# Queries through fp32 loads and on-chip DMA transposes, in an attention kernel followed by a mixture of adapters

## The chip, the cores and the metric

The kernel runs on one core of a Trainium2 chip. The metric is the device time of one execution in microseconds. Before the change the median of three runs is 381.16 us (380.85 to 381.24).

## The reference

```python
# q: 4 x 12288 x 128, kv: 4 x 384 x 32 x 128, w_sr: 128 x 128, all float32
kv_pool = kv.reshape(B, H // 4, 4, W // 4, 4, C).mean(axis=(2, 4))   # 768 keys per batch
k = v = kv_pool.reshape(B, -1, C) @ w_sr
s = (1 / sqrt(C)) * (q @ k.transpose(0, 2, 1))
a = exp(s - s.max(-1)); a /= a.sum(-1) + 1e-09
x = (a @ v).reshape(B * 12288, 128)

logits = x @ w_gate                       # 8 experts
topk = the 2 experts of largest logits
w = softmax of the two logits
delta = sum over the two experts e of w_e * ((x @ A[e]) @ B[e])      # rank 16
return x + delta                          # 49152 x 128, float32
```

## The kernel before, in words

The 49,152 query rows are cut into 96 chunks of 512 rows, 24 chunks a batch. A chunk lies on the chip as 128 partitions by 4 strips (`S`) of 128 columns. Four chunks make a group (`GT` = 2048 rows).

The work of a chunk is a chain. `scores` multiplies the turned queries `qT` (channels on the partitions) by the turned keys `kfT` in three units of two key blocks each (`sg`, in PSUM), and ScalarE takes the exponential into `em`. `attend` multiplies `em` by the values `vx`, which carry the seven differences of the expert logits and a column of ones beside them, into the single accumulator `acc`, one of the four strips at a time. `normalize` takes the reciprocal of the sums (L315) and writes the attention output `xn` (L320). `top` sorts the eight logits of each row on VectorE, `route` and `gates` make the gate weights `gw` on GpSimd, with one tanh on ScalarE between them. `transposes` turns `xn`, so that `down` can multiply by all eight A matrices at once (`h_ps`); `gate` multiplies by `gw` into `hg` on VectorE; `hg` is turned, `up` multiplies by B (`d_ps`), and `finish` adds `xn` and stores the rows.

The main loop (L547) runs over slots `k`, one a chunk, and every engine keeps the order in which the program names its instructions; so does the queue of SP, which issues most transfers. In slot `k` the kernel makes the scores of chunk `k`, attends chunk `k - 1`, normalizes chunk `k - 2`, and lets the chunk of the list `enter[k]` (four or so behind) go through `down` and `gate`. Slots 0 to 7 are an opening written out by hand as a string of steps (L525). Routing is done for two chunks at a time up to chunk 67, in every second slot, and for one chunk from then on.

Chunks up to 67 turn `xn` and `hg` on TensorE, one slot's pair in one PSUM tile `tt_ps`, copied by VectorE into `tts` (L389). Chunks 68 to 89 (`by_dma`) have both turned by one DMA transpose per slot on SP's queue (L407): GpSimd narrows `xn` to bf16 (L403), `gate` writes bf16 beside it, and the transpose takes the two from one tile `turn` to another, 8 blocks of 128 x 128.

Queries of the first eight chunks are loaded in fp32 and turned on TensorE (`load_q`, `turn_q`). For the others GpSimd issues a casting transfer of one group from HBM to HBM (`cast_q`, L80, 512 KB out), and later SP issues a DMA transpose of that group, 16 blocks, into the tile `qT` (`load_qT`, L90).

The keys of the next batch come in loads of 512 KB (`load_kv`, L102), one a slot, and GpSimd adds the 4 x 4 neighbours (`pool_step`, L221 and L223), three sums in every second slot. Then `prepare` turns the sums on TensorE, projects them and makes values and turned keys, one step in each of nine slots of a batch.

Three tiles `kvr` hold raw keys, eight tiles `osb` hold both the first queries and the outputs on their way, and two PSUM tiles `mb` are shared by `tt_ps`, `h_ps`, `d_ps` and the key work.

Of the kernel before, what the change touches and what calls it, by code (L numbers as in the profile page):

```python
# [10 lines left out]
FP32 = mybir.dt.float32  # L11
# [9 lines left out]
def kernel(  # L21
# [32 lines left out]
    qpool = ctx.enter_context(tc.tile_pool(name="qpool", bufs=4))  # L54
# [6 lines left out]
    qdram = ctx.enter_context(tc.tile_pool(name="qdram", bufs=1, space=bass.MemoryType.DRAM))  # L61
# [14 lines left out]
    q_bf, qT, kvr, spare = {}, {}, {}, {}  # L76

    def cast_q(g):
        t = qdram.tile([GT, C], BF16, tag=f"q{g}", name=f"qbf{g}")
        keep(nc.gpsimd.dma_start(t, q[g // NG, (g % NG) * GT:(g % NG + 1) * GT]))  # L80
        q_bf[g] = t

    def load_qT(g):
        if g < B * NG - GC:
            t = qpool.tile([P, GT], BF16, tag="qT", name="qT")
        else:
            if "q" not in spare:
                spare["q"] = kvpool.tile([P, 4, 2, 4 * C], FP32, tag="kvr", name="qTs")
            t = spare["q"][:, g % GC].rearrange("p x c -> p (x c)").bitcast(BF16)
# [17 lines left out]
    q_f = {}  # L107

    def load_q(g, m):
        q_f[g, m] = opool.tile([P, S, C], FP32, tag="osb", name="qf")  # L110
        src = q[0, g * GT:(g + 1) * GT].rearrange("(p j) c -> p j c", p=P)
        keep(nc.sync.dma_start(q_f[g, m], src[:, m * S:(m + 1) * S]))

    def turn_q(g, m, pool, engine):
        if m == 0:
            qT[g] = qpool.tile([P, GT], BF16, tag="qT", name="qT")
# [4 lines left out]
        for i in range(S):  # L121
            mm(ps[:, i], q_f[g, m][:, i], id_f, is_transpose=True,
               start=(i == 0), stop=(i == S - 1))
        o = qT[g][:, m * T:(m + 1) * T].rearrange("p (s t) -> p s t", s=S)
# [33 lines left out]
    for m in range(GC):  # L158
        load_q(0, m)
    load_first(1)  # L160
    load_first(2)
    for m in range(GC):
        load_q(1, m)
# [3 lines left out]
    keep(nc.sync.dma_start(a_f, moe_A.rearrange("e c r -> c e r")))  # L167

# [40 lines left out]

    def prepare(b, adder):  # L210
# [191 lines left out]
    def narrow(k, t):  # L402
        keep(nc.gpsimd.tensor_copy(strip(t, 0)[:, 0], xn[k][:, :, 0:C]))  # L403
# [427 lines left out]
```

## Time and profile before

| | |
|---|---|
| median of three runs | 381.16 us |
| profiled execution, first to last instruction | 379.1 us (its time otherwise is not given) |
| TensorE busy | 368.8 us, 97% |
| VectorE busy | 307.6 us, 81% |
| ScalarE busy | 293.3 us, 77% |
| GpSimd busy | 217.8 us, 57% |
| packets of SP's queue and of GpSimd's queue | 69.8% and 17.0% of 16 DMA engines' span |

Times inside the profile are microseconds from the first instruction. A row of a timeline has the start, the duration, the engine, the line of the kernel, the operation, what it writes and reads, how many instructions the row stands for, and in brackets how long the engine was idle before it and who ended that. PE is TensorE's matmul, PEld its weight load, DVE VectorE, ACT ScalarE, POOL GpSimd, SPq the queue of SP. The ends of matmuls are modelled, so a run of short ones is read from starts. A row of a group has busy time, mean duration in ns, and idle time before. Rows of DMA issues end with the median time from issue to landing.

### The profile page before, as it was taken

What the parts mean: (1) busy time and instruction counts of PE and PEld (TensorE: products, weight loads), DVE (VectorE), ACT (ScalarE), POOL (GpSimd) and SP (SyncE); (2) the same over time, 40 slices, a digit from 0 to 9 for tenths busy, and PEclk for the clock granted to TensorE, in tenths of its full rate; (3) what the DMA queues carried; (4) which work ended last, traced back from release to release, by engine and by line L of the source; (5) the groups of instructions that cost most, each with busy time, mean ns of one, the idle gap of its engine ahead of it and who ended that gap; (6) DMA issues with size and microseconds to landing.
All of it is one profiled execution on the core that took longest, in us unless ns stands there. A gap on an engine that the chain in (4) does not pass through costs nothing.

```text
span 379.1 us, 11473 instructions
## 1 busy us (share of the span) xinstructions
PE 368.8 (97%) x4448; PEld 292.5 (77%) x4448; DVE 307.6 (81%) x925; ACT 293.3 (77%) x368; POOL 217.8 (57%) x493
## 2 busy tenths in 40 slices
PE   8899999999999999999999999999999999999993
PEld 5577788788788887878788887878787777777782
DVE  1447799998989889898989888898988777777785
ACT  1448986776878788787878787777778999999873
POOL 0120468878732387777833267777675666666442
PEclk9999999999999999999999999999999999999998
DMA  7988979999999998997898998989955867777623
GB/s 247 388 291 151 279 184 266 340 224 241 152 213 228 299 278 268 255 235 165 171 201 226 288 239 245 306 233 198 217 137 140 169 163 153 150 205 168 141 86 140
DMA packets 93863, 82.22 MB, mean 217 GB/s; under 512 B 73104, under 2 KB 73872, under 8 KB 93456
## 3 DMA queue, kind: packets, MB, share of 16 engines
q1 hardware_dynamic: 92672, 69.75, 69.8%
q0 software_dynamic: 704, 11.54, 17.0%
q8 instruction: 35, 0.57, 0.6%
q10 hardware_dynamic: 432, 0.20, 0.2%
q14 instruction: 20, 0.16, 0.2%
HBM read 50.53 MB, written 36.70 MB: 230 GB/s over the span
## 4 chain that ended last, share of the span: by engine, by line
PE 91%; DMA 4%; DVE 2%; issue 1%; ACT 1%; SPq 0%; POOL 0%; ACTq 0%; DVEq 0%; POOLq 0%
PE acc L69 35%; PE sg L69 32%; PE tt_ps L69 8%; PE d_ps L69 5%; PE h_ps L69 5%; DMA kvr<-in_kv_dram 4%; PE kpT_ps L69 2%; PE v_ps L69 1%; DVE kvr L135 1%; DVE xn L320 1%; PE kfT_ps L69 1%; DMA out_dram<-osb 1%; PE qT_ps L69 0%; SPq L102 0%; PE tail_ps L69 0%
## 5 line engine op out<-in xcount | busy, mean ns | idle before, releaser
L294 ACT ACTIVATE em<-sg 128x1024 f16<-128x1024 f32 x288 | 282.4, 1022 | 66.8 <-PE sg L69 64.1
L69 PE MATMUL acc<-vx,em 128*128 128x136 f16 x2280 | 166.5, 223 | 0.0
L69 PEld LDWEIGHTS <-em 128*128 128x128 f16 x2304 | 145.2, 98 | 7.7 <-DVE xn L320 0.4
L69 PE MATMUL sg<-qT,kfT 128*128 128x512 bf16 x480 | 142.1, 379 | 0.8 <-ACT em L294 0.7
L320 DVE TENSOR_TENSOR xn<-acc,rinv 128x540 f32<-128x540 f32 x95 | 68.4, 720 | 3.3
L69 PEld LDWEIGHTS <-tts 128*128 128x128 bf16 x564 | 43.0, 98 | 31.6 <-issue 0.4
L223 POOL TENSOR_TENSOR kvr<-kvr 128x512 f32<-128x512 f32 x54 | 67.3, 1270 | 0.1
L352 POOL TENSOR_TENSOR over<-xn,srt 128x64 f32<-128x64 f32 (+1 forms) x120 | 30.9, 278 | 55.4 <-DVE srt L340 55.3
L433 DVE TENSOR_TENSOR osb<-d_ps,xn 128x512 f32<-128x512 f32 x91 | 62.5, 688 | 0.0
L420 DVE TENSOR_TENSOR hg<-h_ps,gw 128x512 bf16<-128x512 f32 x71 | 49.0, 691 | 6.3 <-POOL gw L368 1.2
L389 DVE COPY tts<-tt_ps 128x1024 bf16<-128x1024 bf16 (+1 forms) x73 | 49.0, 672 | 0.0
L69 PEld LDWEIGHTS <-kfT 128*128 128x128 bf16 x576 | 45.3, 98 | 2.7 <-issue 1.0
L315 DVE RECIPROCAL rinv<-acc 128x4 f32<-128x4 f32 x95 | 17.3, 182 | 36.9 <-PE acc L69 35.9
L367 POOL TENSOR_TENSOR gw<-th,over 128x64 f32<-128x64 f32 (+1 forms) x60 | 17.3, 288 | 49.6 <-ACT th L365 47.4
L69 PEld LDWEIGHTS <-xn 128*128 128x128 bf16 x296 | 22.5, 98 | 16.7 <-DVE xn L320 0.4
L340 DVE MAX8 srt<-xn 128x8 f32<-128x8 f32 x380 | 34.4, 152 | 0.1
L69 PE MATMUL sg<-qTs,kfT 128*128 128x512 bf16 x96 | 28.6, 379 | 0.0
L69 PE MATMUL tt_ps<-id_bf,xn 128*128 128x128 bf16 x284 | 27.4, 219 | 0.0
L69 PE MATMUL h_ps<-a_bf,tts 128*128 128x128 bf16 x284 | 27.4, 219 | 0.0
L69 PE MATMUL tt_ps<-id_bf,hg 128*128 128x128 bf16 x280 | 27.1, 219 | 0.0
L69 PE MATMUL d_ps<-b_bf,tts 128*128 128x128 bf16 x276 | 26.7, 219 | 0.1
L358 POOL TENSOR_SCALAR over<-over 128x64 f32<-128x64 f32 (+1 forms) x60 | 19.8, 330 | 5.4
(93 smaller groups left out, 280.7 us busy)
## 6 DMA issues: line engine op xcount, KB each, us to landing
out_dram<-osb SPq DMA_DIRECT2D x94, 256.0 KB, 4.3
kvr<-in_kv_dram SPq DMA_DIRECT2D x45, 512.0 KB, 7.8
qbf<-in_q_dram POOLq DMA_DIRECT2D x22, 512.0 KB, 7.7
qf<-in_q_dram SPq DMA_DIRECT2D x8, 256.0 KB, 7.4
kvr<-in_kv_dram SPq DMA_DIRECT2D x6, 256.0 KB, 7.8
out_dram<-osb SPq DMA_DIRECT2D x3, 128.0 KB, 2.3
turn<-turn SPq DMA_TRANSPOSE x23, 3.1
qT<-qbf SPq DMA_TRANSPOSE x18, 7.4
```

The costliest lines, as they stand in the source:

```text
L69: return keep(nc.tensor.matmul(*a, **k))
L223: keep(adder.tensor_tensor(u[:, lo:hi], u[:, lo:hi], v[:, lo:hi], op=ALU.add))
L294: keep(nc.scalar.activation(em[k][:, 2 * r:2 * r + 2], ps, AF.Exp, bias=0.0, scale=scale))
L315: keep(nc.vector.reciprocal(ri, acc[k][:, :, VC]))
L320: keep(nc.vector.tensor_tensor(x[:, :, 0:VC], acc[k][:, :, 0:VC], ri.unsqueeze(2).broadcast_to([P, S, VC]), op=ALU.mult))
L340: keep(nc.vector.max(srt[k0][:, m, s], xn[k][:, s, C:C + E]))
L352: keep(eng.tensor_tensor(d, lg, so[:, :, i].unsqueeze(2).broadcast_to([P, n, 8]), op=ALU.subtract))
L358: keep(eng.tensor_scalar(mask, mask, 0.0, None, op0=ALU.is_ge))
L367: keep(eng.tensor_tensor(w[:, 0:n], th, mask, op=ALU.mult))
L389: keep(nc.vector.tensor_copy(sb[:, lo:hi], ps[:, lo:hi]))
L420: keep(nc.vector.tensor_tensor(hg[k].rearrange("p s (e r) -> p (s e) r", e=E), hp[k].rearrange("p s (e r) -> p (s e) r", e=E), gw[k0][:, m ...
L433: keep(nc.vector.tensor_tensor(osb, dp[k], xn[k][:, :, 0:C], op=ALU.add))
```

## The change

Queries of all chunks are loaded as fp32, one chunk (256 KB) a transfer, seven slots ahead (`load_q(k + 7)`), into the `osb` tiles. In slot `k` GpSimd narrows the queries of chunk `k + 4` to bf16 into a tile `turn`, and SP turns them by a DMA transpose inside SBUF. From slot 13 on, `gate` also writes its result into that tile, so that one transpose of 8 blocks carries both; the turned `hg` is used by `up` three slots later. In the stage where `xn` was already turned by DMA, the same transpose now has 12 blocks. The casting transfers and the transposes out of HBM are gone, and so are the turns of `hg` on TensorE for the 59 chunks that enter in slots 13 to 71. The tiles for the turns are three sources and six targets in a pool of their own, and from slot 70 five of each inside two `kvr` tiles.

Keys of batches 2 and 3 come in pieces of 256 KB, one a slot from slot 16 to slot 63, with their sums one a slot two slots later (`add_piece`); keys of batch 1 stay as they were. The nine slots of `prepare` move for batches 2 and 3.

```diff
-    def cast_q(g):
-        t = qdram.tile([GT, C], BF16, tag=f"q{g}", name=f"qbf{g}")
-        keep(nc.gpsimd.dma_start(t, q[g // NG, (g % NG) * GT:(g % NG + 1) * GT]))
-        q_bf[g] = t
-
-    def load_qT(g):
...
-        keep(nc.sync.dma_start(t.rearrange("c (j p) -> c j p", p=P),
-                               q_bf[g].rearrange("(p j) c -> p (j c)", p=P), transpose=True))
-        qT[g] = t
...
+    def load_q(k):
+        g, m = k // GC, k % GC
+        q_f[k] = opool.tile([P, S, C], FP32, tag="osb", name="qf")
+        src = q[g // NG, g % NG * GT:(g % NG + 1) * GT].rearrange("(p j) c -> p j c", p=P)
+        keep(nc.sync.dma_start(q_f[k], src[:, m * S:(m + 1) * S]))
...
     def strip(t, i):
...
+        if (t, i) not in strips:
+            if t < TURN + 2:
+                strips[t, i] = tpool.tile([P, 2, S, C], BF16, tag=f"t{i}", name="turn", bufs=(3, 6)[i])
+            else:
...
+                strips[t, i] = spare[i][:, t % 5]
+        return strips[t, i]
 
-    def narrow(k, t):
-        keep(nc.gpsimd.tensor_copy(strip(t, 0)[:, 0], xn[k][:, :, 0:C]))
+    def narrow(t, at, src):
+        keep(nc.gpsimd.tensor_copy(strip(t, 0)[:, at], src))
 
-    def turn_dma(t, *what):
-        lo, hi = (0 if what[0][0] is xT or len(what) == 2 else 1), (2 if what[-1][0] is hgT else 1)
+    def turn_dma(t, lo, *what):
+        hi = lo + len(what)
         keep(nc.sync.dma_start(strip(t, 1)[:, lo:hi].rearrange("c h s p -> c (h s) p"),
                                strip(t, 0)[:, lo:hi].rearrange("p h s c -> p (h s c)"), transpose=True))
...
-    def cast_first():
-        keep(nc.gpsimd.tensor_copy(late, q_f[1, 2][:, 0, 0:1]))
-        for g in (2, 3):
-            cast_q(g)
-        for g in (2, 3):
-            load_qT(g)
+    def turn_pair(k):
+        for i in range(2):
+            narrow(k, i, q_f[k + i])
+        turn_dma(k, 0, (qT, k), (qT, k + 1))
...
+    pieces, adds = {}, {}
+    for b in range(2, B):
+        for n in range(24):
+            pieces[b * NB - 32 + n] = (b, n // 8, n % 8 // 2, n % 2)
...
     def begin(k):
...
+        if k in pieces:
+            load_kv(*pieces[k])
+        if k >= 5 and k + 7 < NCHUNK:
+            load_q(k + 7)
...
+    def add_piece(k):
+        b, h, r, x = pieces.get(k - 2, (0, 0, 0, 0))
+        if r > 0:
+            pool_step(b, h, r - 1, x)
+        for step in (3, 4):
+            b, h, r, x = pieces.get(k - step, (0, 0, 0, 0))
+            if r == 3 and x == 1:
+                pool_step(b, h, step, 0)
...
+    by_queue = [k for t in range(13, TURN + 4) for k in enter[t]]
+    late_up = {}
...
     for k in range(k1, NCHUNK):
...
+        kq = k + 4 if k + 4 < NCHUNK else None
...
         unit()
+        ku = ku + late_up.pop(k, [])
         if kx and not kd and all(x_ in by_dma for x_ in kx):
             down(kx[0])
             todo = []
             for n in kn:
                 normalize(n)
                 if n in by_dma:
-                    narrow(n, k)
-                    todo = [(xT, n)]
+                    narrow(k, 1, xn[n][:, :, 0:C])
+                    todo.append((xT, n))
             tanhs()
+            if kq is not None:
+                narrow(k, 0, q_f[kq])
+                todo.insert(0, (qT, kq))
...
             unit()
-            gate(kx[0], strip(k, 0)[:, 1])
+            gate(kx[0], strip(k, 0)[:, 2])
             todo.append((hgT, kx[0]))
             if len(kx) == 1:
-                turn_dma(k, *todo)
+                turn_dma(k, 3 - len(todo), *todo)
...
         tanhs()
+        todo = []
+        if kq is not None:
+            narrow(k, 0, q_f[kq])
+            todo.append((qT, kq))
...
         for x_ in kx[:1]:
             down(x_)
-            gate(x_)
+            if x_ in by_queue:
+                gate(x_, strip(k, 0)[:, 1 if k < TURN + 2 else 2])
+                todo.append((hgT, x_))
+                late_up[k + 3] = [x_]
+            else:
+                gate(x_)
+        if todo:
+            turn_dma(k, 0, *todo)
...
-        if b + 1 < B and i % 2 == 0 and (8 if b == 0 else 6) <= i <= 20:
-            for _ in range(4 if (b, i) == (0, 18) else 3):
+        add_piece(k)
+        if b == 0 and i % 2 == 0 and 8 <= i <= 20:
+            for _ in range(4 if i == 18 else 3):
                 sums.pop(0)()
```

In the opening, the step `late` (two casting transfers and two transposes out of HBM, for chunks 8 to 15) is replaced by `pair 8`, and a step `pair 10` is added before slot 2; the loads of the queries of chunks 8 to 11 follow the loads of the adapter weights.

More of the change, by code (lines that the diff above doesn't have):

```diff
@@ L167 @@
     keep(nc.sync.dma_start(a_f, moe_A.rearrange("e c r -> c e r")))
+    for k in range(2 * GC, 3 * GC):
+        load_q(k)
     warm = const.tile([P, 1], FP32)
@@ L227, in prepare @@
                 continue
-            sums.append([lambda h=h, step=step, lo=lo: pool_step(h, step, lo, lo + 512)
-                         for step in range(5) for lo in range(0, 1024 if step < 3 else 512, 512)])
+            sums.append([lambda h=h, step=step, x=x: pool_step(b, h, step, x)
+                         for step in range(5) for x in range(2 if step < 3 else 1)])
         st = {}
```

115 lines of the change are left out of this document (50 added, 65 removed), and 4 rows, old and new, of the table opening.

## The prediction

> **What bounds the kernel now.** I read the page first (busy shares, the chain that ended last, the DMA queues), then the timeline of single slots, then sums over three stretches.
>
> ```profile
> PE 368.8 (97%) x4448; PEld 292.5 (77%) x4448; DVE 307.6 (81%) x925; ACT 293.3 (77%) x368; POOL 217.8 (57%) x493
> PE 91%; DMA 4%; DVE 2%; issue 1%; ACT 1%; SPq 0%; POOL 0%; ACTq 0%; DVEq 0%; POOLq 0%
> q1 hardware_dynamic: 92672, 69.75, 69.8%
> q0 software_dynamic: 704, 11.54, 17.0%
> ```
>
> The chain is 91% TensorE and no other engine holds it for long; the two queues together fill 87% of the DMA engines' time, but they are off the chain after the opening. How much of TensorE's busy time is really path is read from starts, since the ends are modelled. Timeline of TensorE, a slot of the plain stage and one of the stage that already turns by DMA:
>
> ```profile
> 206.19 0.39 PE L69 MATMUL tt_ps<-id_bf,xn 128*128 128x128 bf16 x4
> 206.42 0.39 PE L69 MATMUL tt_ps<-id_bf,hg 128*128 128x128 bf16 x4
> 206.64 0.59 PE L69 MATMUL sg<-qT,kfT 128*128 128x512 bf16 x2
> ...
> 209.80 0.39 PE L69 MATMUL tt_ps<-id_bf,xn 128*128 128x128 bf16 x4
> ...
> 301.46 0.39 PE L69 MATMUL h_ps<-a_bf,turn 128*128 128x128 bf16 x4
> ...
> 304.63 0.28 PE L69 MATMUL h_ps<-a_bf,turn 128*128 128x128 bf16 x2
> ```
>
> A plain slot lasts 209.80 - 206.19 = 3.61 us, a slot without either group of turns 304.63 - 301.46 = 3.17. The four turns of hg start at 206.42 and the next group at 206.64: they cost 0.22, not the 0.39 of their busy time, and two such groups are exactly the difference between the stages. TensorE issues without a hole in both, so four turns fewer are 0.22 less, as long as nobody else is late. The three stretches in which the change acts (slots 8 to 21, 22 to 71, 72 to 91; a slot starts at its reciprocal of L315):
>
> ```profile
> 51.22:101.68 50.46, 50.46 (x653) 41.54 (x652) 46.60 (x137) 36.98 (x45) 41.35 (x69) 1.00 0.99 252
> 101.68:288.12 186.44, 186.44 (x2355) 150.69 (x2354) 166.13 (x479) 146.35 (x176) 112.34 (x220) 1.00 0.97 227
> 288.12:351.82 63.70, 63.62 (x765) 49.30 (x764) 47.91 (x161) 60.59 (x80) 41.93 (x140) 1.00 0.73 165
> ```
>
> After the length stand busy PE, PEld, DVE, ACT, POOL, the granted clock (1.00) and the DMA share. A mean slot is 3.60, 3.73 and 3.19 us.
>
> **The change part by part.**
>
> Gain on TensorE: the 59 chunks that enter in slots 13 to 71 lose four turns each, 59 x 0.22 = 13.0 us if every cover holds. Their VectorE copy shrinks too:
>
> ```profile
> L389 DVE COPY tts<-tt_ps 128x1024 bf16<-128x1024 bf16 x68 | 47.0, 691 | 0.0
> L389 DVE COPY tts<-tt_ps 128x512 bf16<-128x512 bf16 x5 | 2.1, 416 | 0.0
> ```
>
> That is 0.27 less per slot on an engine busy 166.13 of 186.44: no gain of its own, but it keeps VectorE (3.05 of 3.51) behind TensorE. ScalarE, 146.35 / 50 = 2.93 of 3.51, has room as well.
>
> GpSimd loses the issue of 22 casting transfers and gains one narrowing per chunk (88, four of them in the opening, where it is idle between 30 and 40 us). Its rows by form, and one round of two slots on it:
>
> ```profile
> L403 POOL CAST turn<-xn 128x512 bf16<-128x512 f32 x22 | 13.4, 610 | 10.7 <-DVE xn L320 10.7
> L80 POOL DMA_DIRECT2D qbf<-in_q_dram x22 | 12.7, 579 | 0.0
> L223 POOL TENSOR_TENSOR kvr<-kvr 128x512 f32<-128x512 f32 x54 | 67.3, 1270 | 0.1
> 30.00:40.00 10.00, 10.00 (x116) 7.78 (x115) 6.67 (x29) 9.40 (x13) 0.00 (x0) 1.00 0.74 129
> 53.01 0.32 POOL L367 TENSOR_TENSOR gw<-th,over 128x64 f32<-128x64 f32 x1 [2.21 <-ACT th L365]
> 53.40 0.32 POOL L368 TENSOR_TENSOR gw<-gw,over 128x64 f32<-128x64 f32 x1
> 53.68 3.73 POOL L223 TENSOR_TENSOR kvr<-kvr 128x512 f32<-128x512 f32 x3
> 57.37 0.57 POOL L352 TENSOR_TENSOR over<-xn,srt 128x64 f32<-128x64 f32 x2
> ...
> 59.38 0.32 POOL L367 TENSOR_TENSOR gw<-th,over 128x64 f32<-128x64 f32 x1 [0.59 <-ACT th L365]
> ```
>
> In slots 22 to 71 GpSimd is busy 2.25 of 3.73; with 0.61 more, and the rarer cast issue gone, about 2.7 of 3.51: covered. In slots 8 to 21 it is not: there the key sums of batch 1 still come three at a time, and the round is closed (gates, sums, routing, the tanh on ScalarE, gates again: 59.38 - 53.01 = 6.37 us with 0.59 of waiting, the length of two slots). The change puts two narrowings into each round: 14 x 0.61 = 8.5, two sums of new pieces (slots 20, 21) 2.5, less six cast issues 3.5: 41.35 + 7.5 = 48.9 us of work. Seven rounds keep their 0.59 wait for the tanh: 4.1. So the stretch lasts about 53.0, against 50.46 now and 50.46 - 9 x 0.22 = 48.5 for TensorE alone. I take +2.5; the ends are -2.0 (cover holds) and +5 (the four-sum round at slot 18 and keys(2) at slot 21, which waits for the last sums, are not made up). If a gate is late, VectorE is late with it (in order), then the accumulator and TensorE.
>
> Slots 22 to 71: 50 x 0.22 = -11.0.
>
> SP and the DMA engines. Per slot SP now issues a query load, a store, a turn and in slots 16 to 63 a 256 KB key piece; a turn's wait for the gate, late in the slot, holds up the next slot's loads behind it, and a query load waits until the slot before has narrowed the query whose buffer it takes. The key pieces carry the same bytes as the 512 KB loads, in twice the issues, and are added in as many sums; keys and values of a batch move to other slots with the same work: nothing for either.
>
> ```profile
> 302.87 1.24 SPq L407 DMA_TRANSPOSE turn<-turn  x1
> 304.20 0.53 SPq L434 DMA_DIRECT2D out_dram<-osb  x1
> turn<-turn SPq DMA_TRANSPOSE x1, 2.4
> turn<-turn SPq DMA_TRANSPOSE x16, 3.1
> qTs<-qbf SPq DMA_TRANSPOSE x4, 6.6
> q1 hardware_dynamic: 19447, 8.59, 74.0%
> 10.00:20.00 10.00, 8.19 (x55) 5.69 (x54) 4.09 (x8) 5.05 (x6) 1.77 (x1) 1.00 1.03 400
> ```
>
> The two rows for turns are of 4 blocks of 128x128 (window 283 to 285) and of 8 (300 to 350), the third of 16 out of HBM; the 74.0% is the queue in 300 to 350, the last row the loads of the opening (share 1.03, 400 GB/s). SP: 1.24 + 3 x 0.53 + four gaps of 0.09 = 3.2 us of a 3.51 us slot: it fits. DMA: 0.74 x 3.16 = 2.34 us for one store and one 8-block turn, two more 256 KB transfers at 400 GB/s 0.66 each: 3.65 by packet time, which overlaps (the share reached 1.03 above). I charge nothing for slots 22 to 71, because queries are loaded seven slots ahead, turned four ahead, and gated activations wait three slots for a turn of 3.1; without that cover see the third rival. The casts' trip through HBM leaves; nothing waited for it, so no gain.
>
> Slots 72 to 91. TensorE's work is unchanged here, but the turn becomes 12 blocks and waits for a narrowing more:
>
> ```profile
> 301.45 0.72 DVE L320 TENSOR_TENSOR xn<-acc,rinv 128x540 f32<-128x540 f32 x1
> 302.24 0.61 POOL L403 CAST turn<-xn 128x512 bf16<-128x512 f32 x1 [0.52 <-DVE xn L320]
> 302.95 0.25 POOL L367 TENSOR_TENSOR gw<-th,over 128x32 f32<-128x32 f32 x1
> 303.29 0.25 POOL L368 TENSOR_TENSOR gw<-gw,over 128x32 f32<-128x32 f32 x1
> ```
>
> Now the turn is issued at 302.87. The query's narrowing is behind the gates on GpSimd: 303.54 to about 304.19, so the turn goes at 304.24, 1.37 later. Its landing: 2.4 for 4 blocks, 3.1 for 8, so 3.8 for 12 by the same step; the far end is halfway to the 16-block row, 4.85. The reader is the h_ps group two slots on, 301.46 + 2 x 3.16 = 307.78; 304.24 + 3.8 + 0.1 = 308.14 is 0.36 late per two slots, 0.18 a slot, 20 x 0.18 = +3.6 us. Ends: 0 and +14 (4.85 gives 0.7 a slot). I take the nearest rows, 4 and 8 blocks out of SBUF.
>
> The Trainium skill (Advanced Engine Details and Errata, section X-Bar Transpose (TRN2)) says that transposing DMAs run as fast as plain ones, 350 to 400 GB/s. By that four more blocks cost 0.35 us, the landing is 3.45, this term is about nil and the time 372.7. The trace disagrees: 131 KB more took 0.7 us, 187 GB/s.
>
> Sum: +2.5 - 11.0 + 3.6 = -4.9. The profiled execution spans 379.1 us, and 2.06 more lie around it in the median of 381.16; no other time of it is given. 379.1 - 4.9 = 374.2, plus 2.06: **376.3 us**.
>
> **Rivals.**
> First, every cover holds: slack between gate and next reciprocal absorbs the rounds, and the turns land in time. -13.0: 368.2 us. For it: TensorE never waits today. Against: 48.9 us of GpSimd work in 48.5.
> Second, slower: the 12-block turn lands late, because a turn of more than 8 blocks is generated in two parts, as the 16-block row suggests (6.6, not the 4.5 of the step). At 4.85 the price is 14.1: +2.5 - 11.0 + 14.1 = +5.6, 386.8 us. It decides from a landing of 4.3 (20 x 0.425 eats the other 8.5). Against it: those 16 blocks came out of HBM.
> The Trainium skill's VectorE: DVE Perf Modes (section The three transpose paths) gives 390 ns for one block on TensorE and 1309 by DMA, and its rules advise TensorE where PSUM will do. This trace agrees on the latency (0.22 of path against 2.4 to landing).
> Third, the DMA queue paces slots 22 to 63 at its packet time, 3.65: 42 x 0.08 = 3.4 gained there and 1.8 after it, +2.5 and +3.6 lost: 382.1 us. For it: 87% full today. Against: the two queues become one and the casts' second trip goes.
> Fourth, the change does not do what it says: another engine holds slots at 3.73, and 381.2 + 2.5 + 3.6 = 387.3. VectorE and ScalarE rows speak against it.
>
> **How the numbers follow.** Forecast 0.42 (its own range 373 to 380.5), first 0.14, second 0.24, third 0.14, fourth 0.06. A measurement can tell about 0.2%, that is 380.4 to 381.9. Of the forecast 0.39 is faster, 0.01 same, 0.02 slower; of the third 0.03, 0.04, 0.07. Faster: 0.39 + 0.14 + 0.03 = 0.56; same 0.01 + 0.04 = 0.05; slower 0.02 + 0.24 + 0.07 + 0.06 = 0.39. The range goes from the first rival to the second, 368 to 387.
>
> **What would show it.** Plain slots of 3.39 between slots 24 and 71; hg turns gone there and copies of 0.42; GpSimd nearly full from 51 to 104 us with VectorE's gate waiting for gw; SP's turn at 2.8 us into a late slot and slots of 3.3 there. It is wrong if plain slots stay above 3.5 with TensorE waiting for a DMA of turn, or if late slots exceed 3.6.

## The result, and the profile after

The changed kernel takes 394.5 us (median of four runs, 392.3 to 398.0) against 381.0 us (four runs of the kernel before, 380.1 to 381.2): 1.037 times the time before, 95% interval 1.031 to 1.043. The forecast was 376.3, with a range from 368 to 387. Here and below, runs more than 1.5% above the fastest of their kernel are left out of medians and ratios. Its profiled execution is the longest of the four, 398.0 us with a span of 396.2. From the page of the changed kernel (busy times, SP's queue with packets, MB and share, the chain by engine), then the rows of the waits (idle time, times, mean):

```profile
PE 362.3 (91%) x4143; PEld 281.1 (71%) x4212; DVE 292.8 (74%) x924; ACT 295.9 (75%) x368; POOL 255.3 (64%) x558
...
q1 hardware_dynamic: 140352, 100.56, 100.7%
...
PE 53%; DMA 27%; POOL 8%; DVE 5%; issue 4%; ACT 2%; SPq 0%; POOLq 0%; ACTq 0%
```

```profile
PEld L69 <- DMA turn<-turn: 26.9, 25, 2.7
...
PE h_ps L69 <- DMA turn<-turn: 8.2, 7, 2.4
PE d_ps L69 <- DMA turn<-turn: 7.5, 7, 2.1
...
PEld kpT_ps L69 <- POOL kvr L205: 2.4, 1, 2.4
```

TensorE's work is smaller, as meant, but the chain, 91% TensorE before, is 53% TensorE and 27% DMA: TensorE's weight loads wait for turns 25 times, and its matmuls stand for 8.2 + 7.5 us behind such waits. (The share of a queue counts the time that its packets take, waiting included: a window shown at the end has 150.2% with 0.19 MB moved in 2 us. So 100.7% is not a full queue by itself.) The three stretches of the prediction, in busy times by windows:

```profile
50.48:106.91 56.43, 50.17 (x607) 40.37 (x616) 43.24 (x135) 37.79 (x45) 48.40 (x80) 0.98 1.12 284
106.91:292.45 185.54, 179.05 (x2120) 140.62 (x2154) 152.90 (x479) 146.89 (x176) 131.14 (x252) 1.00 1.12 272
292.45:368.03 75.58, 65.55 (x751) 49.56 (x764) 49.16 (x161) 61.74 (x80) 52.78 (x162) 0.98 1.04 237
```

Against 50.46, 186.44 and 63.70 before: slots 8 to 21 take 6.0 us more, slots 22 to 71 only 0.9 less, slots 72 to 91 take 11.9 more. With -0.7 ahead of slot 8 and +0.9 behind slot 91 these are the 17.1 us between the spans. The granted clock of 0.98 in the first and third stretch does not make the difference: e5 and g2 below take 74.3 and 75.2 us for slots 72 to 91 at 1.00.

**A plain slot that nothing disturbs.** Timeline of the changed kernel:

```profile
118.63 0.18 DVE L301 RECIPROCAL rinv<-acc 128x4 f32<-128x4 f32 x1 [0.25 <-PE acc L69]
...
118.86 0.39 PE L69 MATMUL tt_ps<-id_bf,xn 128*128 128x128 bf16 x4
119.08 0.59 PE L69 MATMUL sg<-turn,kfT 128*128 128x512 bf16 x2
119.12 1.02 ACT L280 ACTIVATE em<-sg 128x1024 f16<-128x1024 f32 x1 [0.49 <-PE sg L69]
...
119.74 0.52 PE L69 MATMUL acc<-vx,em 128*128 128x136 f16 x6
...
120.19 0.38 PE L69 MATMUL sg<-turn,kfT 128*128 128x512 bf16 x1
```

The turns of hg are gone and the group of xn's turns is 0.22 us long (118.86 to 119.08). But six matmuls of `acc` begin at 119.74 and the third scores only at 120.19; they need one of the two `sg` tiles, which ScalarE's first exponential frees at 119.12 + 1.02 = 120.14. TensorE meets that limit because the 0.22 us that used to stand ahead of it is gone. The median plain slot is 3.48 us, not 3.39.

**A plain slot that waits.** Timeline of SP's queue, VectorE's gate and TensorE, and the landing of the turn issued at 156.68:

```profile
153.00 1.56 SPq L400 DMA_TRANSPOSE turn<-turn  x1
...
153.38 0.69 DVE L414 TENSOR_TENSOR turn<-h_ps,gw 128x512 bf16<-128x512 f32 x1 [0.21 <-POOL gw L354]
...
154.61 0.77 SPq L87 DMA_DIRECT2D kvr<-in_kv_dram  x1
...
155.75 0.35 SPq L96 DMA_DIRECT2D qf<-in_q_dram  x1
...
156.21 0.36 SPq L428 DMA_DIRECT2D out_dram<-osb  x1
...
156.68 1.54 SPq L400 DMA_TRANSPOSE turn<-turn  x1
...
162.85 0.40 PE L69 MATMUL d_ps<-b_bf,turn 128*128 128x128 bf16 x4 [0.52 <-DMA turn<-turn]
```

```profile
DMA to landing us min/median/max: 6.1/6.1/6.1
```

The gate that this turn carries ended at 153.38 + 0.69 = 154.07 (the next one starts only at 156.73), but SP issued it at 156.68, 2.6 us later: SP's four issues fill a whole slot, 3.68 us from one turn to the next. The turn lands at 162.8, and TensorE, which uses it three slots after the gate, starts at 162.85. The three slots left 8.1 us between the gate's end and the time at which d_ps was due (162.2, a slot of 3.48 behind the one at 158.69), and 2.6 + 6.1 is more. Worked out over all turns in slots 22 to 63, the issue comes 2.6 us (median, at most 4.5) behind the last input, SP is busy 3.32 us of a slot, and a turn lands 4.9 us after its issue (3.1 in the late stage before): the middle of these still fits, the upper ends do not.

**A late slot that waits.** Timeline, and the landing of the turn issued at 321.88:

```profile
318.96 0.18 DVE L301 RECIPROCAL rinv<-acc 128x4 f32<-128x4 f32 x1 [0.88 <-PE acc L69]
...
321.21 0.61 POOL L396 CAST turn<-qf 128x512 bf16<-128x512 f32 x1
...
321.88 2.05 SPq L400 DMA_TRANSPOSE turn<-turn  x1
...
328.11 0.40 PE L69 MATMUL h_ps<-a_bf,turn 128*128 128x128 bf16 x4 [2.35 <-DMA turn<-turn]
```

```profile
DMA to landing us min/median/max: 6.2/6.2/6.2
```

SP has no lag here: the narrowing ends at 321.82, the turn goes at 321.88, 2.92 us into the slot. It lands at 328.1, and h_ps has waited 2.35 us.

### The profile page after: what moved, and what is told of

Same layout as the page of the kernel before. It is cut to its first block, busy times and chain, and to the rows that moved or that the text cites. A ratio compares the mean times of both kernels' runs of the same rounds, so it can differ in the third digit from the quotient of the medians.

```text
span 396.2 us, 11303 instructions
## 1 busy us (share of the span) xinstructions
PE 362.3 (91%) x4143; PEld 281.1 (71%) x4212; DVE 292.8 (74%) x924; ACT 295.9 (75%) x368; POOL 255.3 (64%) x558
## 3 DMA queue, kind: packets, MB, share of 16 engines
q1 hardware_dynamic: 140352, 100.56, 100.7%
## 4 chain that ended last, share of the span: by engine, by line
PE 53%; DMA 27%; POOL 8%; DVE 5%; issue 4%; ACT 2%; SPq 0%; POOLq 0%; ACTq 0%
PE acc L69 22%; DMA turn<-turn 19%; PE sg L69 17%; DMA kvr<-in_kv_dram 8%; PE h_ps L69 4%; PE d_ps L69 4%; POOL kvr L205 3%; PE tt_ps L69 3%; POOL turn L396 2%; DVE osb L427 1%; DVE xn L306 1%; ACT em L280 1%; DVE rinv L301 1%; PE v_ps L69 1%; POOL gw L353 1%
## 5 line engine op out<-in xcount | busy, mean ns | idle before, releaser
L69 PE MATMUL acc<-vx,em 128*128 128x136 f16 x2280 | 168.4, 224 | 1.0 <-DVE xn L306 0.2
L69 PE MATMUL sg<-turn,kfT 128*128 128x512 bf16 x464 | 144.1, 381 | 0.2 <-ACT em L280 0.2
L205 POOL TENSOR_TENSOR kvr<-kvr 128x512 f32<-128x512 f32 (+1 forms) x72 | 86.0, 1202 | 0.4
L414 DVE TENSOR_TENSOR turn<-h_ps,gw 128x512 bf16<-128x512 f32 x81 | 55.8, 689 | 20.3 <-PE h_ps L69 8.7
L396 POOL CAST turn<-qf 128x512 bf16<-128x512 f32 x88 | 53.6, 609 | 13.9 <-DMA turn<-turn 7.0
L69 PEld LDWEIGHTS <-turn 128*128 128x128 bf16 x412 | 29.8, 98 | 45.8 <-DMA turn<-turn 26.9
L69 PEld LDWEIGHTS <-kfT 128*128 128x128 bf16 x576 | 47.3, 98 | 5.8 <-issue 1.3
L69 PE MATMUL d_ps<-b_bf,turn 128*128 128x128 bf16 x324 | 31.6, 220 | 8.3 <-DMA turn<-turn 7.5
L69 PEld LDWEIGHTS <-tts 128*128 128x128 bf16 x328 | 24.7, 97 | 17.6
L375 DVE COPY tts<-tt_ps 128x512 bf16<-128x512 bf16 (+1 forms) x72 | 32.4, 450 | 0.3 <-PE tt_ps L69 0.3
```

The source lines that it names most:

```text
L69: return keep(nc.tensor.matmul(*a, **k))
L205: keep(nc.gpsimd.tensor_tensor(u, u, v, op=ALU.add))
L375: keep(nc.vector.tensor_copy(sb[:, lo:hi], ps[:, lo:hi]))
L396: keep(nc.gpsimd.tensor_copy(strip(t, 0)[:, at], src))
L414: keep(nc.vector.tensor_tensor(hg[k].rearrange("p s (e r) -> p (s e) r", e=E), hp[k].rearrange("p s (e r) -> p (s e) r", e=E), gw[k0][:, m ...
```

## The experiments

Slots are cut at the reciprocals, as in the prediction. Times are medians; span and stretches are those of one profiled execution each, all in us. The time of an execution is about 1.8 us longer than its span, so e4 and e6 were profiled in an execution 6 us above and 4 us below the time given.

| run | time | span | slots 8-21 | 22-63 | 64-71 | 72-91 |
|---|---|---|---|---|---|---|
| before | 381.0 | 379.1 | 50.4 | 155.7 | 30.8 | 63.7 |
| changed | 394.5 | 396.2 | 56.4 | 156.5 | 29.0 | 75.6 |
| e1 queries narrowed first, late | 390.5 | 387.7 | 52.9 | 155.9 | 29.0 | 71.7 |
| e2 quarter of query bytes | 386.4 | 382.9 | 53.1 | 152.4 | 29.0 | 69.7 |
| e3 hg on TensorE | 394.5 | 391.6 | 53.0 | 156.9 | 29.9 | 72.8 |
| e4 four slots for hg | 388.3 | 393.0 | 53.3 | 157.5 | 29.5 | 73.0 |
| e5 third scores later | 394.3 | 393.9 | 53.5 | 158.5 | 28.5 | 74.3 |
| e6 early narrowing on ScalarE | 392.4 | 386.2 | 52.1 | 152.9 | 28.7 | 73.0 |
| e8 = e1 + e2 + e5 | 377.7 | 375.9 | 52.2 | 148.6 | 29.7 | 66.0 |
| f1 quarter of key bytes | 394.7 | 391.9 | 54.5 | 154.3 | 29.0 | 74.2 |
| g2 keys in 512 KB | 393.0 | 391.7 | 54.9 | 154.2 | 29.0 | 75.2 |
| c1 late stage from chunk 80 | 387.4 | 385.0 | 52.0 | 157.2 | 28.8 | 70.0 |
| g5 candidate | 386.4 | 385.0 | 51.7 | 154.3 | 28.3 | 72.4 |

The four runs of the changed kernel go from 392.3 to 398.0, so where turns are late a stretch of one execution is read to two or three us: in slots 22 to 63 e1 and e6 run the changed kernel's own code and take 155.9 and 152.9. c1 and g5 contain e1, e5 and e6.

**Queries narrowed first in the late stage**

```diff
             down(kx[0])
             todo = []
+            if kq is not None:
+                narrow(k, 0, q_f[kq])
+                todo.append((qT, kq))
             for n in kn:
...
             tanhs()
-            if kq is not None:
-                narrow(k, 0, q_f[kq])
-                todo.insert(0, (qT, kq))
```

> Changed kernel, but in slots 72 to 91 GpSimd narrows the queries ahead of xn and of the gates, so the 12-block turn is no longer behind that narrowing. Theory ORDER (the turn of the late stage is issued about 1.4 us too late, as the prediction had it): most of the 12.9 us that the late stage lost comes back, 382 to 385 us, and h_ps no longer waits there. Theory DMA (the DMA engines are full, and a turn lands late whenever it is issued): the turn is issued earlier but lands about as late; 0 to 4 us come back, 390 to 395 us, and TensorE still waits for the turn behind each 16 KB instruction fetch.

390.5 us. The turn is issued 2.24 us into the late slot instead of 2.99 (medians), 0.75 of the 1.37 that the prediction had counted for the narrowing, and slots 72 to 91 are 3.9 us shorter than in the changed kernel's profile, 2.4 shorter than the mean of the seven runs with that stage unchanged (74.0). This is theory DMA's side: the turn, issued earlier, still lands 4.7 us later and is still waited for.

**A quarter of the query bytes**

```diff
-        keep(nc.sync.dma_start(q_f[k], src[:, m * S:(m + 1) * S]))
+        n = 1 if k >= 20 else S
+        keep(nc.sync.dma_start(q_f[k][:, 0:n], src[:, m * S:m * S + n]))
```

> Changed kernel, but for chunks 20 to 95 only one of the four strips of the queries is loaded (64 KB instead of 256 KB) and the narrowing reads that strip four times: three quarters of these chunks' queries are left out of the computation, every instruction on the engines keeps its size, only the bytes of the loads change. Theory DMA: 192 KB less a slot (about 0.5 us of the queue) lets a turn catch up after a fetch; the stalls of TensorE on turns go in slots 22 to 91, some 5 us in slots 22 to 71 and 10 to 13 in the late stage, 377 to 381 us. Theory ORDER (turns are issued late or their own length is too long): within 2 us of the changed kernel, 392 to 396.

386.4 us: between the two theories, 8 us less than the changed kernel where theory DMA promised 14 to 17. Issues of turns with their median landing in the late stage (292 to 350 us) of the changed kernel, of e1 and of e2:

```profile
turn<-turn SPq DMA_TRANSPOSE x15, 5.1
```

```profile
turn<-turn SPq DMA_TRANSPOSE x17, 4.7
```

```profile
turn<-turn SPq DMA_TRANSPOSE x17, 3.9
```

With 192 KB a slot less beside it, a 12-block turn lands in 3.9 us, which is the 3.8 of the prediction; beside the full loads it takes 4.7 to 5.1 (4.6 over the whole stage of the changed kernel). What it says of the other half: the issue stays at 2.89 us into the slot, and 2.89 + 3.9 is still late at times. Slots 22 to 71 of e2, by windows:

```profile
103.67:285.06 181.39, 181.18 (x2155) 141.64 (x2154) 153.05 (x480) 146.63 (x176) 131.75 (x252) 0.99 1.01 225
```

TensorE is busy for 181.18 of 181.39 us and waits for no turn: with the queries' bytes alone reduced, the late turns of this stretch are gone in this execution, and it takes 5.0 us less than before the change.

**hg on TensorE again**

```diff
-    by_queue = [k for t in range(13, TURN + 4) for k in enter[t]]
+    by_queue = []
```

> Changed kernel, but hg is turned on TensorE again in slots 13 to 71 (queries still by their own 4-block DMA turn; the late stage as in the changed kernel). Theory DMA: four blocks a slot less in the queue, so the d_ps waits go (5 to 6 us), the plain slot is 3.61 again (+6.5 us over 50 slots), the late stage keeps its loss of about 13: 392 to 397 us in all. Theory SLACK (the three slots given to the gated activations are what costs, also by its backlog later): the loss of the late stage shrinks as well and the kernel goes to 381 to 386 us.

394.5 us, theory DMA. Undoing this part costs nothing and gains nothing: d_ps no longer waits, the plain slot is 3.61 again, and the late stage keeps its loss. Sixteen undisturbed plain slots (32 to 47) of this kernel, of e2 (hg by DMA), and of e8 (hg by DMA, third scores later):

```profile
141.30:200.91 59.61, 59.61 (x753) 48.20 (x752) 53.28 (x152) 46.82 (x56) 42.84 (x81) 1.00 0.99 243
```

```profile
141.18:198.62 57.44, 57.44 (x689) 45.00 (x688) 48.76 (x152) 46.82 (x56) 42.80 (x81) 1.00 1.03 234
```

```profile
138.61:194.47 55.86, 55.28 (x678) 44.49 (x688) 47.90 (x153) 47.64 (x56) 42.75 (x81) 1.00 1.09 241
```

So taking hg's turns off TensorE is worth (59.61 - 57.44) / 16 = 0.14 us a slot, and 0.10 more lies behind the exponential: together 0.23, the 0.22 of the prediction.

**Four slots for hg**

```diff
-                late_up[k + 3] = [x_]
+                late_up.setdefault(k + (4 if k < 68 else 3), []).append(x_)
```

> Changed kernel, but up takes the turned hg of a chunk four slots after its gate instead of three (slots 13 to 67). Theory TRANSIENT (a turn is late for one or two slots behind an instruction fetch, then the queue recovers): the waits of d_ps in slots 16 to 70 go, 6 to 8 us less, 386 to 389 us. Theory BACKLOG (the queue never recovers, its lag is the whole slack whatever that is): the waits move to the scores, which take the queries of the same turn four slots later, 0 to 2 us less, 392 to 395 us.

388.3 us from 387.1 and 389.5, about the range of theory TRANSIENT; but two more runs took 394.7 and 394.8, the range of BACKLOG, and the profiled one is of these. In it the lag of a turn's issue behind its data grows with the slack, from 2.6 to 4.3 us (median, slots 22 to 63), GpSimd waits 24.4 us in all for the tiles that turns still hold, and slots 22 to 71 are no shorter. This run does not decide between the two; nor was it tried whether more tiles would let the fourth slot count.

**Third scores later**

```diff
-        if k >= 13:
-            unit()
-            n0 = 1
-        else:
-            attend(ka[0], 1)
-            n0 = 2
+        attend(ka[0], 1)
+        n0 = 2
+        if k >= 13:
+            unit()
```

> Changed kernel, but from slot 13 the third unit of scores stands behind two strips of attention instead of one, in the plain slots (up to 71). Theory EXP (with hg's turns gone, the third scores reach TensorE before ScalarE has freed one of the two score tiles, which is why a plain slot is 3.48 and not 3.39): the undisturbed plain slot becomes 3.39 to 3.41 us, 3.5 to 4.5 us less over slots 22 to 71, 390 to 391 us. Rival, DMA pace (plain slots are held at 3.48 by the transfers): the median plain slot stays at 3.47 to 3.50 and the time within 1.5 us of the changed kernel's 394.5.

394.3 us. Each theory is right on one count. The median plain slot is 3.385 us, so it was the exponential that held it at 3.48. But the time is the same: slots 22 to 63 take 158.5 us, because what each slot gains is waited away in late turns (33 waits of 33.5 us in all, 25 of 26.9 before). A faster TensorE only reaches the turns sooner.

**Early narrowing on ScalarE**

```diff
+            if k < 22:
+                keep(nc.scalar.copy(strip(k, 0)[:, 0], q_f[kq]))
+            else:
+                narrow(k, 0, q_f[kq])
```

> Changed kernel, but in slots 8 to 21 ScalarE narrows the queries instead of GpSimd. Theory GPSIMD (the sums of batch 1 and the narrowings overfill GpSimd there, as the prediction had it): slots 8 to 21 take 50 to 51.5 us instead of 53 (the other runs with GpSimd narrowing gave 52.9 to 53.3, the profiled execution of the changed kernel 56.4), the wait of keys(2) for the sums at slot 21 goes, 391 to 393 us in all. Rival (late turns hold this stretch): 53 to 56 us there as before, and TensorE waits for a turn.

392.4 us. Slots 8 to 21 take 52.1, just over the range of theory GPSIMD; the wait of keys(2) for the sums falls from 2.4 to 1.4 us but does not go, and TensorE waits for two late turns, as the rival had it. GpSimd's narrowing is part of this stretch's loss; part stays.

**Order, bytes and scores together**

The edits of e1, e2 and e5 in one kernel.

> Changed kernel with three edits at once, which act on separate stretches: queries narrowed first in slots 72 to 91, a quarter of the query bytes loaded from chunk 20 on (three quarters of these queries are left out of the computation), third scores later in slots 13 to 71. The first alone left 71.7 us for slots 72 to 91, the second alone 69.7; the kernel before took 63.7. Theory TWO CAUSES (turn issued 1.4 late and lands 1.5 late, either alone eats the slack of two slots): slots 72 to 91 take 63.5 to 65.5 us, slots 22 to 71 some 177, in all 375 to 378 us. Rival LENGTH (12 blocks are too long in themselves, whatever their issue and the other transfers): 68 us or more for slots 72 to 91, and 380 us or more in all.

377.7 us, 0.994 times the kernel before (0.990 to 0.998). The late stage of e1, e2 and of this kernel:

```profile
288.03:359.68 71.65, 65.36 (x765) 48.52 (x764) 49.09 (x162) 61.71 (x80) 53.34 (x163) 1.00 1.12 256
```

```profile
285.06:354.73 69.67, 65.11 (x765) 48.56 (x764) 48.93 (x161) 61.44 (x80) 52.89 (x162) 1.00 0.96 206
```

```profile
281.54:347.53 65.99, 63.48 (x751) 48.93 (x764) 48.44 (x162) 60.98 (x80) 53.13 (x163) 1.00 1.08 225
```

65.99 is 0.5 over the range of theory TWO CAUSES and below LENGTH's 68: 12 blocks are not too long in themselves. Slots 22 to 71 take 178.3, where 177 was expected. With both covers restored and the third scores moved, the kernel comes out at 377.7, near the forecast of 376.3, but only with three quarters of the later queries left out.

**A later start of the late stage**

```diff
-    SOLO, TURN = NCHUNK - 6, NCHUNK - 28
+    SOLO, TURN = NCHUNK - 6, NCHUNK - 16
```

with the edits of e1, e5 and e6.

> A version with all queries computed: the changed kernel with queries narrowed first in the late stage, third scores later, ScalarE narrowing in slots 8 to 21, and the stage with 12-block turns begun twelve chunks later (chunk 80 instead of 68), so that the query loads end four slots into it. Theory DMA (three transfers of 256 KB, or two and 12 blocks, fill the DMA engines in the stages as cut now; a plain slot without key pieces has room): slots 72 to 83 take 3.40 each instead of 3.58, slots 8 to 21 about 50.5, slots 22 to 71 about 180, in all 375 to 380 us, below the kernel before. Rival (the loss follows the queries turned by DMA wherever they are): TensorE goes on waiting for turns in slots 72 to 83 and the time stays above 385 us.

387.4 us, above the kernel before and above what was expected. Slots 72 to 83, with two 256 KB transfers and an 8-block turn, run without a stall at 40.62 / 12 = 3.385 us, although the DMA share is 1.11:

```profile
288.10:328.72 40.62, 40.20 (x497) 32.11 (x504) 34.52 (x110) 35.67 (x43) 19.59 (x53) 1.00 1.11 234
```

The loss does not follow the turned queries wherever they are; it needs a third large transfer beside them, or the 12 blocks. Slots 22 to 63, with key pieces, keep theirs (157.2).

**The hg part alone, on the kernel before**

```diff
+    def turn_hg(k, src):
+        o = tpool.tile([P, S, P], BF16, tag="t1", name="turn", bufs=5)
+        keep(nc.sync.dma_start(o, src.rearrange("p s c -> p (s c)"), transpose=True))
+        hgT[k] = o
...
-            gate(x_)
+            if x_ in by_queue:
+                g_ = tpool.tile([P, S, P], BF16, tag="t0", name="turn", bufs=3)
+                gate(x_, g_)
+                turn_hg(x_, g_)
+                late_up[k + 3] = [x_]
```

> The kernel before with one part of the change alone: from slot 13 to 71 hg is turned by a 4-block DMA transpose of its own on SP and used three slots later; queries and keys as before. Theory QUERIES (the 4 blocks fit when the queries' narrowing and fp32 loads are not there): the quiet plain slot falls by the 0.13 us seen in the changed kernel, 59 x 0.13 = 7.7, about 373 us. Theory DMA (the engines were 97% busy in slots 22 to 71 before, four blocks more a slot fill them): part of the gain is lost in waits of d_ps for turns, 376 to 384 us. With no gain at all (384 or more) the move of hg is harmful by itself.

> As the run of the hg part alone, and the third scores of a plain slot stand behind two strips of attention. Theory EXP: quiet plain slots of 3.39 (before: 3.61), 4 to 5 us less than with the hg part alone wherever no turn is late; 368 to 379 us, whichever of the two theories holds for that run. Rival, DMA pace: the quiet slot is shorter but waits for turns grow by as much, the same time as with the hg part alone within 1.5 us.

421 to 434 us over the eight runs of the two, far outside every expectation (the second is 1.127 times the kernel before, 1.122 to 1.131). Undisturbed plain slots are 3.48 in the first and 3.38 in the second, but every few slots one takes 6 to 12 us. Timelines of the first, SP and GpSimd's issue, and TensorE:

```profile
118.00 1.23 SPq L405 DMA_TRANSPOSE turn<-turn  x1
119.32 1.59 SPq L440 DMA_DIRECT2D out_dram<-osb  x1
121.00 4.22 SPq L405 DMA_TRANSPOSE turn<-turn  x1
125.31 0.58 SPq L103 DMA_DIRECT2D kvr<-in_kv_dram  x1
```

```profile
117.44 0.57 POOL L81 DMA_DIRECT2D qbf<-in_q_dram  x1
...
125.77 0.61 PE L70 MATMUL d_ps<-b_bf,turn 128*128 128x128 bf16 x4 [3.95 <-DMA turn<-turn]
```

A casting transfer is issued at 117.44 and lands at 125.29, 7.8 us later (also the median of the twelve between 110 and 260 us). The turn for which TensorE waits is the one issued at 118.00: it lands at 125.72, when the cast is out, and TensorE starts at 125.77. The turn behind it, at 121.00, takes SP 4.22 us instead of 1.23. Of the turns issued between 110 and 260 us, the 22 with a cast in flight land in 7.6 us (median), the 10 others in 5.4, and all nine waits of d_ps over 2 us are for turns with a cast in flight. The queries' own transposes of 16 blocks are a rival, since they come as often as the casts; nine turns that have one in flight and no cast land in 5.6. So the casts, harmless before because nothing waited for a transfer, go with turns that are late for a reader three slots on; no run takes the casts alone away. The two parts of the change need each other: next to the casts the hg part is far worse than next to the fp32 loads that replace them.

**The hg part from slot 60 on, on the kernel before**

The same edit with `range(60, TURN + 4)`, and third scores later.

> The kernel before with hg turned by DMA only in slots 60 to 71 and the third scores behind two strips: no key loads there, but six loads of turned queries of 16 blocks fall into slots 61 to 67. If the DMA engines have room, 12 x 0.22 = 2.6 us less, 377.5 to 378.5 us; if the query turns crowd it, a turn or two is late and the time is 380 to 383 us.

386.6 us, 1.015 (1.012 to 1.018): slots 64 to 71 take 34.2 us instead of 30.8, slower than the 380 to 383 of the crowded case. Two waits of d_ps for turns, 3.4 and 1.7 us, are more than all of it. No cast is in flight with either turn; a query transpose of 16 blocks is, with the first.

**A quarter of most key bytes**

```diff
-            keep(nc.sync.dma_start(kvr[b, h][:, r, x], src[:, :, x * 4 * C:(x + 1) * 4 * C]))
+            n = C if b > 1 and r > 0 else 4 * C
+            keep(nc.sync.dma_start(kvr[b, h][:, r, x, 0:n], src[:, :, x * 4 * C:x * 4 * C + n]))
```

> Changed kernel, but three of four rows of the key pieces of batches 2 and 3 are loaded by a quarter (64 KB instead of 256 KB, the sums read that quarter four times), so most of these keys are left out of the computation; the queries are loaded whole and every instruction on the engines keeps its size. It takes 144 KB a slot out of slots 16 to 63 and nothing out of slots 72 to 91. Theory DMA (it is the sum of the bytes that makes turns late): slots 22 to 63 run at the quiet 3.59 us a slot, some 151 us instead of 156.5, while slots 72 to 91 keep 72 to 76 us; 387 to 390 us. Rival (the query loads themselves, or the instruction fetches whatever else is moving): waits for turns in slots 22 to 63 stay, 392 to 396 us.

394.7 us, inside the rival's range. Slots 32 to 55 do run at the quiet 3.59 (the mean with their key work), but slots 22 to 63 take 154.3, 2.2 less instead of 5.7, and the lag of the issues stays at 2.5 us. Since the changed kernel's own code took from 152.9 (e6) to 156.5 there, 2.2 us less is not clear of the scatter.

**Key pieces issued by GpSimd; keys in 512 KB**

```diff
-            keep(nc.sync.dma_start(kvr[b, h][:, r, x], src[:, :, x * 4 * C:(x + 1) * 4 * C]))
+            eng = nc.gpsimd if b > 1 else nc.sync
+            keep(eng.dma_start(kvr[b, h][:, r, x], src[:, :, x * 4 * C:(x + 1) * 4 * C]))
```

> Changed kernel, but the key pieces of batches 2 and 3 (slots 16 to 63) are issued by GpSimd instead of SP; all bytes and all turns stay. In the changed kernel SP is busy 3.32 us of a slot in slots 22 to 63, and a turn is issued 2.6 us (median) after its last input is ready. Theory SP (the queue of SP issues the turns late): SP falls to some 2.7 us a slot, turns are issued within 0.5 us of their data, slots 22 to 63 take the quiet 3.59 us each, 151 us instead of 156.5, and the time is 387 to 390 us. Theory DMA (the bytes): the same waits as before, 392 to 396 us.

```diff
-            load_kv(*pieces[k])
+            b_, h_, r_, x_ = pieces[k]
+            if x_ == 0:
+                load_kv(b_, h_, r_, None)
```

> Changed kernel with one part of the change undone: the keys of batches 2 and 3 come as 512 KB in every second slot again instead of 256 KB in each (same bytes, same sums). Theory SP: half of those issues go, 0.3 us a slot of SP's time, so the turns' lag behind their data falls from 2.6 to 1 us or less and the waits for turns in slots 22 to 63 mostly go: 387 to 391 us. Theory DMA: no fewer bytes, 392 to 396 us.

402.8 us (400.0 and 405.7; 1.059 times the kernel before, 1.046 to 1.071; two more runs took 407.9, the profiled one, and 419.2) and 393.0 us. The first refutes theory SP in its simple form: the lag of the issues falls from 2.6 to 0.1 us as it said, and the kernel is slower; the transfers now take longer. Median landings between 110 and 260 us, changed kernel and g1:

```profile
qf<-in_q_dram SPq DMA_DIRECT2D x40, 256.0 KB, 4.4
turn<-turn SPq DMA_TRANSPOSE x40, 4.9
```

```profile
qf<-in_q_dram SPq DMA_DIRECT2D x39, 256.0 KB, 5.9
...
turn<-turn SPq DMA_TRANSPOSE x39, 6.7
```

In the second, half of the key issues are gone and SP is nearly as busy as before, 3.27 us of a slot: the issues take longer. The lag falls to 1.8 us, not to 1, and a turn lands in 5.7. So SP's time is not a price list: the issue of an 8-block turn took 1.24 in the late stage before and 1.53 here, and in both runs relief of SP came with longer landings. The Trainium skill (DMA: Bandwidth & Descriptors, section Issuing engines are not separate DMA queues) says that transfers of all issuing engines share the same 16 DMA engines, and that a second issuer saves only the issue time. The first run agrees with both as far as they go: the lag falls, and SP's query loads land in 5.9 us instead of 4.4 beside GpSimd's; the time is 8 us longer all the same.

**Two candidates with everything computed**

g2 with e1, e5, e6, and in the late stage the queries' narrowing on VectorE (g5); the same with the query loads of chunks 79 to 95 issued by GpSimd (g4).

```diff
-                narrow(k, 0, q_f[kq])
+                keep(nc.vector.tensor_copy(strip(k, 0)[:, 0], q_f[kq]))
...
+        eng = nc.gpsimd if k >= 79 else nc.sync
+        keep(eng.dma_start(q_f[k], src[:, m * S:(m + 1) * S]))
```

> A version with everything computed: keys in 512 KB, third scores later, ScalarE narrowing in slots 8 to 21, and in the late stage the queries narrowed first and by VectorE, which frees GpSimd. By theory SP slots 8 to 21 take 51 to 52, slots 22 to 71 176 to 179, slots 72 to 91 (SP busy 3.1 of 3.16 there) 69 to 72, in all 376 to 381 us. By theory DMA 384 to 390 us.

> As the candidate before it in this call, and the query loads of chunks 79 to 95 are issued by GpSimd. Theory SP: in slots 72 to 88 SP falls from 3.1 to 2.6 us a slot and slots 72 to 91 take 64 to 67 us, 371 to 376 us in all. Theory DMA: slots 72 to 91 stay at 69 us or more.

386.4 and 392.6 us, both as theory DMA had it: slots 72 to 91 take 72.4 and 76.8. g5 is the best version with everything computed that these runs gave on the changed kernel's plan, 8 us below it and 1.015 times the kernel before (1.013 to 1.017). None beat the kernel before.

## Why the prediction was wrong

In the profiled execution, slots 8 to 21 lost 6.0 us where the sum had 2.5, slots 22 to 71 gained 0.9 where it had 11.0, and slots 72 to 91 lost 11.9 where it had 3.6.

**The step that failed first: "I charge nothing for slots 22 to 71", with SP's "it fits" and 3.65 us of packet time against a slot of 3.51 put aside as overlapping.** SP's sum of 3.2 us took an 8-block turn and transfers at the durations of a queue with room. In the changed kernel the turn's issue takes 1.53 and SP 3.32 of 3.48, issues come 2.6 us late, and a turn lands in 4.9 instead of 3.1; the cover of three slots is gone at times. In e2, where no turn is late there, slots 22 to 71 gain 5.0 us; in the changed kernel late turns leave 0.9 of it. e5 shows it best: a slot shorter by 0.10 changes the time by nothing. The third rival (the DMA queue paces slots 22 to 63, at 3.65) comes nearest, since the queue does hold TensorE; but it is no steady pace. Most plain slots run at 3.48, and the loss stands in a few late turns. That the stretch measured 156.54 / 42 = 3.73 a slot, no gain at all, is near its number partly by luck: slots with key work, of 3.6 to 4.0 us without any wait, are in this mean.

**Gain on TensorE, 0.22 a slot.** The size is right, 0.23, but only with the third scores moved (e8); as the change stands 0.14, because the exponential's hold on the score tiles was next in line. The prediction looked at VectorE and ScalarE by their busy time per slot, which does not show that loop.

**GpSimd in slots 8 to 21, +2.5.** The size came out in four runs, e1 to e4: 52.9 to 53.3 us, that is +2.5 to +2.9. Most of it stands in one place, the wait of keys(2) for the sums, which the prediction had kept for its upper end: slot 21 takes 6.28 us in e2 and 3.99 before, the 13 slots ahead of it 46.8 and 46.5. From the changed kernel's profile, its transposes of the last sums of batch 1:

```profile
104.42 0.44 PE L69 MATMUL kpT_ps<-id_f,kvr 128*128 128x128 f32 x2 [2.21 <-POOL kvr L205]
```

The 6.0 of the profiled execution has two late turns on top, 3.1 us of TensorE's time, which the prediction did not have in this stretch; f1 and g2, at 54.5 and 54.9, have such turns too. e6 took back about one microsecond of the term, so the narrowings are only part of its cause, and the rest is open.

**Slots 72 to 91, +3.6.** The place and the issue are right: 1.37 later was worked out, to 3.01 us into the slot, and the median is 2.99. The landing is the term that was mis-sized: 3.8 forecast, 4.6 (median over the stage) measured, with late ones of 6.2. The 3.8 is what a 12-block turn takes when the queries' loads are small (3.9 in e2); the prediction priced the blocks and left out of the landing the 256 KB query load that the change puts beside them in every slot. The step from a late landing to microseconds was too small as well: e2 has nearly the prediction's own issue and landing, 2.89 and 3.9, and still loses 6.0 us, with six waits of h_ps for turns, 4.6 us in all. One landing for all slots leaves out the late ones, up to 5.7 there. Over the seven kernels in which this stage is the same (the changed one, e3 to e6, f1, g2: 72.8 to 75.6) the loss is 9 to 12 us. The second rival gave this size and side (14.1 from a landing of 4.85, deciding at 4.3), but with another cause, a turn generated in two parts; e2 and e8 speak against that, since the same 12 blocks land in 3.9 to 4.2.

**First and fourth rival.** Neither holds: covers did not hold, and the slot did fall where nothing was late. The fourth's other engine was there, though: ScalarE's exponential held the plain slot, at 3.48 and not at 3.73.

**What would show it.** Two of its signs of failure came: TensorE waiting for a DMA of turn, and late slots over 3.6 (75.58 / 20 = 3.78). Plain slots over 3.5 came in the mean, 3.71.

**What stays open.** How SP's stretching issues and the DMA engines share the blame in slots 22 to 63 is not settled. Two runs leave no wait of TensorE for a turn there: a quarter of the query bytes (e2) and hg back on TensorE (e3). Fewer key bytes and larger pieces (f1, g2) leave 154.3 and 154.2 us, inside the scatter of unchanged code, and another issuer (g1) made it worse. In slots 72 to 91 the early issue (e1) and the fewer bytes (e2) each took back part, and only both together, in e8 beside e5's edit, brought the stretch to within 2.3 us of the kernel before.

## What to carry to other kernels

A transfer that nothing waits for and the same transfer with a reader three slots on have different prices: before moving work from an engine to a DMA, sum what each stage's queue will carry beside it, at landings measured under that load, and ask for slack well above them. When such a sum comes out above the slot, as 3.65 against 3.51 did, it is a warning that the term is not nothing; it is no pace either, since c1's slots 72 to 83 ran without a stall at a DMA share of 1.11. Behind an engine that is busy 97% there can be a second limit, here 0.1 us a slot above what the change should have reached, and only the order of single instructions showed it.

## What the runs showed of the hardware that was not expected

In b1 a DMA transpose with a casting transfer in flight (packets of 16 KB: 11.54 MB in 704) landed in 7.6 us instead of 5.4 (medians), and one such issue took 4.22 us instead of 1.23: a few large packets on another queue went with a delay far beyond the transpose's own bytes. The fetches of instructions seem to do the same on a smaller scale: in the changed kernel 33 packets of 16 KB (0.54 MB) come some 12 us apart. A window of two microseconds of the changed kernel with one of them (40 slices of 0.05 us: DMA share, GB/s; then packets by queue), while the turn issued at 156.68 is in flight:

```profile
DMA  9588698999965967999999990020002000200010
GB/s 440 159 256 266 189 189 220 159 492 174 113 133 133 169 159 164 148 108 102 72 61 51 36 5 0 0 41 0 0 0 41 0 0 0 41 0 0 0 41 0
...
q1 hardware_dynamic: 529, 0.19, 150.2%
q8 instruction: 1, 0.02, 2.9%
```

The throughput falls to almost nothing for the last 0.8 us although the turn lands only at 162.8 and SP has been issuing another load since 159.70; that looks like engines waiting for the one that is behind. Over the turns after 100 us of that execution, those with a fetch from 2 us ahead of their issue to their landing land in 5.3 us (median of 41), the others in 4.5 (32). A longer landing makes such a meeting likelier; with a window of fixed length, from 2 us before the issue to 3 us after it, the two are 5.2 (31) and 4.5 (42). No run changes the fetches alone, so this is a correlation and was not shown to be the cause.
